# Sliding-window attention into a squared-ReLU FFN on one core: eight of the transposes of x moved from TensorE to transposing DMAs on ScalarE's queue

## The chip, the cores and the metric

The kernel runs on one core of one Trainium2 chip. The metric is device time in microseconds (us). Times of runs are medians over whole executions; times of single instructions come from one profiled execution and are counted from the start of its span. Engines: TensorE (PE), VectorE (DVE), ScalarE (ACT), GpSimd (POOL), SyncE (SP), which here only issues DMAs. ACT can issue DMAs too; such an instruction stands in the same queue as ACT's computing instructions, in order.

## The reference

Causal attention with a window of 64 over 8 sequences of 576 tokens (8 heads of 64), its output laid out as 4608 tokens x 512, and a feed-forward layer on it.

```python
scores = scale * q @ k.T                     # q, k, v: (8, 8, 576, 64)
mask = (rel >= 0) & (rel < 64)               # rel = query position - key position
attn = softmax(where(mask, scores, -1e9))
x = (attn @ v).transpose(0, 2, 1, 3).reshape(4608, 512)
h = maximum(x @ w_in, 0)                     # w_in: 512 x 2048
out = (h * h) @ w_out                        # w_out: 2048 x 512
```

## The kernel before

**Blocks.** The tokens are worked in nine blocks of 512. Blocks 0 to 7 are the first 512 tokens of each sequence; block 8 (`g == B`) holds the last 64 tokens of all eight. A block's attention has four units, one for each pair of heads: `(g, hp)` with `hp` 0 to 3.

**One unit.** `Sc` makes the scores of a unit on TensorE into one of two PSUM tiles, `at0` or `at1` (L287), and ACT takes their exponential into `pm` (L294). `M` applies the mask on DVE (L301). `AV` multiplies by v on TensorE into the same `at` tile (L317), `N` divides by the sums on DVE and leaves x of the unit as `xs` in SBUF (L327; three buffers). `X` transposes xs into `xT`, which the feed-forward layer needs with the features on the partitions: four TensorE transposes into the unit's own `at` tile (L343) and a copy by ACT from there (L124, called with the name `copy`). For block 8 only, `X` issues one transposing DMA on SP instead (L335).

**Feed-forward layer.** `F1(g, f)` computes 128 of the 2048 hidden features: four matmuls into `hps` (L357; two PSUM tiles), maximum with 0 by DVE into `hr` (L360; three buffers), square by ACT into h2 (L361). The second product, from block 2 on, is done with seven products of half size in each direction in place of eight (`L2S`, L444), with sums formed on DVE beforehand (`S_sum`, L420, and `T_sum`). The products go to two PSUM tiles, `chain` and `side`; ACT empties them into `osb` (L458) or DVE adds them there (L461). A product that writes `chain` anew has to wait for the eviction of the one before.

**Stages.** After a start that is written out, the loop `for n in range(1, NBLK)` makes stages 1 to 8. Stage n does the second product of block n, the first product of block n+1 and the attention of block n+2. The matmul groups of the two products alternate in a list `fill` of 30 groups, and the steps of the attention are put ahead of given groups with `put(i, ...)`. Two units run side by side (`t` = 0, 1), the first pair of a block from group 8 or 9 of its stage on, the second pair from group 19 or 20 (17 in stage 6). The order of all instructions is written by hand (`tc.manual_schedule()`); every engine runs its own instructions in that order.

**Loads.** `next_part`, called between groups, loads 128 tokens of q, k or v (SP, L211; L214 and L218 for block 8), has POOL cast them to fp16 (L126), and, for q and k, transposes them with a DMA on SP (`transpose_part`, L244), four parts behind the loading. In stage n it brings in block n+3: 12 loads and 8 transposes, for block 8 more (20 parts, 12 of them transposed). The stores of the output (L382) stand in SP's queue as well.

**Semaphores.** DMAs of SP and ACT use eight semaphores in turn (DMAHW0 to 7). What an instruction has to wait for is worked out from the tiles that it reads and writes when the program is built.

Of the kernel before, what the change touches and what calls it, by code (L numbers as in the profile page):

```python
# [15 lines left out]
def kernel(  # L16
# [13 lines left out]
    nc = tc.nc  # L30
    B, H, S, D = q.shape
# [22 lines left out]
    ps_tr = ctx.enter_context(tc.tile_pool(name="ps_tr", bufs=1, space=bass.MemoryType.PSUM))  # L54
# [67 lines left out]
    def copy(engine, out, in_):  # L122
        if engine is nc.scalar:
            engine.activation(out=out, in_=in_, func=AF.Copy, scale=1.0)  # L124
        else:
            engine.tensor_copy(out=out, in_=in_)  # L126
# [120 lines left out]
    pm, av, xs, xT = {}, {}, {}, {}  # L247
# [49 lines left out]
    def M(g, hp):  # L297
        p = pm[g, hp]
        m0 = 1 if g == B else 0
        m = mask[:, m0:m0 + 8, :].rearrange("p j r -> p (j r)")  # L300
        nc.vector.tensor_tensor(out=p[:], in0=p[:], in1=m.unsqueeze(1).broadcast_to([P, 2, 512]),  # L301
                                op=ALU.min)
# [24 lines left out]
        nc.vector.tensor_tensor(out=x[:].rearrange("p j h d -> p h j d"), in0=a[:, :, :, 0:D],  # L327
                                in1=rden[:].unsqueeze(3).broadcast_to([P, 2, 4, D]), op=ALU.mult)

    def X(g, hp, engine=nc.scalar, pool=ps_tr, tag="tr", own=None):  # L330

        if g not in xT:
            xT[g] = xtpool.tile([P, DMC, 512], FP16, name="xT", tag="xT")
        if g == B:
            nc.sync.dma_start_transpose(out=xT[g][:, hp, :].rearrange("p (j t) -> p j t", j=4),  # L335
                                        in_=xs[g, hp][:].rearrange("p j h d -> p (j h d)"))
            return
        if own is not None:
            tr = at_ps[own][:, 0, :].bitcast(FP16).rearrange("p (a b) -> p a b", a=2)
        else:  # L340
            tr = pool.tile([P, 2, 512], FP16, name="xtr", tag=tag)
        for jp in range(4):
            nc.tensor.transpose(out=tr[:, 0, jp * P:(jp + 1) * P], in_=xs[g, hp][:, jp, :, :],  # L343
                                identity=ident[:])
        copy(engine, xT[g][:, hp, :], tr[:, 0, :])
# [4 lines left out]
    def F1(g, f, pool=ps_f1, tag="f1", into=None):  # L350
        if g not in h2:
            h2[g] = h2pool.tile([P, FFC, 512], FP16, name="h2", tag="h2")
        hps, done = open_f1.pop((g, f), (None, 0))
        if hps is None:
            hps = into if into is not None else pool.tile([P, 512], FP32, name="hps", tag=tag)
        for c in range(done, DMC):
            nc.tensor.matmul(hps[:], w_in_sb[:, c, f * P:(f + 1) * P], xT[g][:, c, :],  # L357
                             start=(c == 0), stop=(c == DMC - 1))
        hr = opool.tile([P, 512], FP32, name="hr", tag="hr")
        nc.vector.tensor_scalar(out=hr[:], in0=hps[:], scalar1=0.0, scalar2=None, op0=ALU.max)  # L360
        nc.scalar.activation(out=h2[g][:, f, :], in_=hr[:], func=AF.Square)  # L361
# [26 lines left out]
    def F2(g, ts, quarter, pool, tag, into=None):  # L388
        if quarter == 0:
            f2[g, ts] = into if into is not None else pool.tile([P, 512], FP32, name="ops", tag=tag)  # L390
        for f in range(4 * quarter, 4 * quarter + 4):
            nc.tensor.matmul(f2[g, ts][:], h2[g][:, f, ts * P:(ts + 1) * P], w_out_sb[:, f, :],  # L392
                             start=(f == 0), stop=(f == FFC - 1))
        if quarter == 3:
            osb = opool.tile([P, DM], FP32, name="osb", tag="osb", bufs=5)
            nc.scalar.activation(out=osb[:], in_=f2[g, ts][:], func=AF.Copy, scale=OUT_SCALE)
            to_store.append(lambda: store(g, ts, osb))
        if quarter == 1:
            while to_store:
                to_store.pop(0)()  # L400
# [21 lines left out]
    def T_sum(k):  # L422
        if k == 1:
            minus(t_of(1), b_of(0, 1), b_of(0, 0))
        elif k == 2:
            minus(t_of(2), b_of(1, 1), t_of(1))
        elif k == 3:
            minus(t_of(3), b_of(1, 1), b_of(0, 1))
        else:
            minus(t_of(4), b_of(1, 0), t_of(2))  # L430

    def S_sum(g, k, s):
        if k == 1:
            minus(s_of(1, s), a_of(g, 1, 0, s), a_of(g, 1, 1, s), ALU.add)
        elif k == 2:
            minus(s_of(2, s), s_of(1, s), a_of(g, 0, 0, s))
        elif k == 3:
            minus(s_of(3, s), a_of(g, 0, 0, s), a_of(g, 1, 0, s))
        else:
            minus(s_of(4, s), a_of(g, 0, 1, s), s_of(2, s))  # L440
# [74 lines left out]
    with tc.manual_schedule():  # L515
# [18 lines left out]
        dve, pool, act = nc.vector, nc.gpsimd, nc.scalar  # L534
# [127 lines left out]
        def A(g, hp, i=1):  # L662
            AV(g, hp, i)
            N(g, hp)
# [38 lines left out]
        for n in range(1, NBLK):  # L703
            g = seq[n]
            last = n == NBLK - 1
            one = None if last else seq[n + 1]
            if n == 1:
                second = [lambda ts=ts, i=i: F2(g, ts, i, None, None, into=(chain, side)[ts % 2])
                          for ts in range(4) for i in range(4)]
            elif last:  # L710
                more = [ps_f1.tile([P, 512], FP32, name="more", tag="f1") for _ in range(2)]
                banks = [(more[0][:, 0:HC], more[1]), (chain[:, 0:HC], side)]
                second = [lambda p=p, s=s: L2S(g, p, s, banks[s])
                          for p, s in ((1, 0), (2, 0), (1, 1), (6, 0), (2, 1), (5, 0), (7, 0),
                                       (6, 1), (3, 0), (4, 0), (5, 1), (7, 1), (3, 1), (4, 1))]
            else:
                second = [lambda p=p, s=s: L2S(g, p, s, (chain[:, 0:HC], side))
                          for s in range(2) for p in ORDER]
            first = [] if last else [lambda f=f: F1(one, f) for f in range(FFC)]
            order = ("22222222" + 8 * "112" if n == 1 else  # L720
                     "2" * 14 if last else
                     "1212121212121211" + "21212121121122")
            a, b = iter(first), iter(second)
            fill = [next(a if c == "1" else b) for c in order]
            at = {}

            def put(i, *work):
                at.setdefault(i, []).extend(work)

            if n == 1:  # L730
                put(0, lambda: Sc(g2, 3), lambda: A(g2, 2))
                put(2, lambda: M(g2, 3))
                put(3, lambda: X(g2, 2, own=1))
                put(5, lambda: A(g2, 3))
                put(7, lambda: X(g2, 3, own=1))
                for i, k in ((1, 1), (3, 2), (6, 3), (8, 4)):
                    put(i, lambda k=k: T_sum(k))
            else:
                for i, k, s in (((0, 1, 1), (0, 2, 1), (2, 4, 0), (3, 3, 1), (4, 4, 1)) if last else
                                ((2, 4, 0), (4, 1, 1), (6, 2, 1), (9, 3, 1), (13, 4, 1))):  # L740
                    put(i, lambda k=k, s=s: S_sum(g, k, s))
            if not last:
                end = len(fill) - 1
                put(24 if n == 1 else 17, lambda: S_sum(one, 3, 0))
                put(end if n == 1 else end - 1, lambda: S_sum(one, 1, 0))
                put(end, lambda: S_sum(one, 2, 0))
            base = 4 * (n + 2)
            for i, two in zip((11, 21) if n == 1 else (9, 20) if n == 2 else (9, 17) if n == 6 else (8, 19),
                              (units[base:base + 2], units[base + 2:base + 4])):
                for t, u in enumerate(two):  # L750
                    if u is not None:
                        put(i, lambda u=u, t=t: Sc(*u, i=t))
                        put(i + 3 + t, lambda u=u: M(*u))
                        put(i + 6, lambda u=u, t=t: A(*u, i=t))
                        put(i + (7 if u[0] == B else 8 + t), lambda u=u, t=t: X(*u, own=t))
            for i, group in enumerate(fill):
                for work in at.pop(i, []):
                    work()
                total = 12 + (30 * (n - 1) + i + 1) * (len(load_list) - 12) // 140
                while done < total and (parts_left or pending):  # L760
                    next_part()
                    done += 1
                group()
            assert not at, at.keys()
# [30 lines left out]
```

## Time and profile before

| | |
|---|---|
| Median of 3 runs | 302.12 us (301.2 to 302.79) |
| The profiled execution: time, span | 301.14 us, 298.8 us |
| Busy: PE, DVE, ACT, POOL | 289.0, 216.6, 169.2, 126.0 us |
| Transposes of xs on PE (L343) | 128 matmuls, 88 of them into `at` |
| Copies xT by ACT from `at` (L124) | 22, 586 ns each |
| Transposing DMAs, all on SP | 52 of q and k (L244), 4 of xs (L335) |
| DMA queue 1 | 143504 packets, 55.14 MB |

The span is the time from the first to the last instruction of the program; the rest of an execution's time lies around it. A line of a view gives line number, engine, operation, output <- input. A queue's own instructions (SPq, ACTq), DMA issues above all, are not counted as busy. In the listings by line, three numbers with slashes are the shortest, median and longest duration in ns. In a timeline the first number is the start in us, the second the length; xN means that N like instructions stand together.

### The profile page before, as it was taken

The numbers are of one execution on the slowest core, as the hardware profiler recorded it, in microseconds if no ns is written. First come the engines' busy times: TensorE is split into PE (matmuls) and PEld (weight loads), VectorE is DVE, ScalarE is ACT, GpSimd is POOL, SyncE is SP. The second block draws the span as 40 slices with busy tenths as digits, with TensorE's granted clock in tenths as the row PEclk, the third lists the DMA queues.
The fourth block names the chain that finished last, engine by engine and source line by source line (L and its number), as shares of the span: only waits on it lengthen the run. The fifth ranks groups of instructions, "written<-read, shape, count | busy, mean of one in ns | idle before, by whom it ended". The sixth has DMA issues, their size and how long they took to land.

```text
span 298.8 us, 7389 instructions
## 1 busy us (share of the span) xinstructions
PE 289.0 (97%) x2908; PEld 181.0 (61%) x2908; DVE 216.6 (72%) x380; ACT 169.2 (57%) x291; POOL 126.0 (42%) x214
## 2 busy tenths in 40 slices
PE   7999998999999999999999999999999999999994
PEld 5544544545444456666666666666666666766783
DVE  4677527588866777968797879787878688875651
ACT  3657745587466557565656565656565655444521
POOL 4568849963383367339326634723241000000001
PEclk9999999999999999999999999999999999999999
DMA  7999999999999995999899999999994023200016
GB/s 217 249 344 378 391 335 270 308 204 172 190 256 174 199 218 107 206 191 219 164 210 244 197 178 224 173 202 208 220 205 145 2 37 105 74 36 35 2 70 140
DMA packets 143874, 56.05 MB, mean 188 GB/s; under 512 B 127904, under 2 KB 136352, under 8 KB 143840
## 3 DMA queue, kind: packets, MB, share of 16 engines
q1 hardware_dynamic: 143504, 55.14, 85.8%
q8 instruction: 22, 0.36, 0.5%
q0 software_dynamic: 96, 0.26, 0.4%
q10 hardware_dynamic: 240, 0.20, 0.3%
q14 instruction: 12, 0.10, 0.1%
HBM read 38.80 MB, written 9.44 MB: 161 GB/s over the span
## 4 chain that ended last, share of the span: by engine, by line
PE 77%; DVE 1%; ACT 1%; issue 1%; DVEq 0%
PE hps L357 36%; PE chain L444 15%; PE side L444 11%; PE at L317 3%; PE at L287 3%; PE side L392 2%; PE chain L392 2%; PE more L444 2%; PE at L343 1%; DVE hr L360 0%; PE tr L256 0%; ACT h L361 0%; PE hps L373 0%; ACT xT L124 0%; PE at L357 0%
## 5 line engine op out<-in xcount | busy, mean ns | idle before, releaser
L361 ACT ACTIVATE h<-hr 128x512 f16<-128x512 f32 x144 | 90.2, 631 | 93.8 <-DVE hr L360 93.7
L357 PE MATMUL hps<-xT,w_in_sb 128*128 128x512 f16 x560 | 138.7, 379 | 0.2
L360 DVE TENSOR_SCALAR hr<-hps 128x512 f32<-128x512 f32 x143 | 97.0, 687 | 40.8 <-PE hps L357 38.3
L357 PEld LDWEIGHTS <-w_in_sb 128*128 128x128 f16 x564 | 52.7, 98 | 46.7 <-issue 1.4
L444 PEld LDWEIGHTS <-hsum 128*128 128x128 f16 x448 | 43.2, 98 | 13.2
L126 POOL CAST v_ev<-st_v 128x512 f16<-128x512 f32 x32 | 22.6, 706 | 41.7 <-DMA st_v<-in_v_dram 41.7
L444 PEld LDWEIGHTS <-h 128*128 128x128 f16 x336 | 32.6, 98 | 9.3
L126 POOL CAST k<-st_k 128x512 f16<-128x512 f32 x31 | 21.7, 703 | 35.0 <-DMA st_k<-in_k_dram 31.9
L294 ACT ACTIVATE pm<-at 128x1024 f16<-128x1024 f32 x35 | 34.2, 1020 | 2.8 <-PE at L287 2.8
L386 POOL DMA_DIRECT2D out_dram<-osb x2 | 1.3, 632 | 66.1 <-ACT osb L458 66.1
L444 PE MATMUL chain<-wsum,hsum 128*128 128x256 f16 x208 | 27.0, 273 | 0.0
L327 DVE TENSOR_TENSOR xs<-at,rden 128x512 f16<-128x512 f32 x36 | 24.9, 692 | 1.2
L301 DVE TENSOR_TENSOR pm<-pm,mask 128x1024 f16<-128x1024 f16 x32 | 23.8, 755 | 1.8 <-ACT pm L294 1.8
L420 DVE TENSOR_TENSOR hsum<-h 128x1024 f16<-128x1024 f16 x28 | 20.4, 729 | 6.0 <-ACT h L361 5.7
L126 POOL CAST q<-st_q 128x512 f16<-128x512 f32 x27 | 18.5, 706 | 12.4 <-DMA st_q<-in_q_dram 7.2
L235 POOL CAST v_od<-st_v 64x512 f16<-64x512 f32 x30 | 21.4, 713 | 1.6
L392 PEld LDWEIGHTS <-h 128*128 128x128 f16 x128 | 11.8, 98 | 12.8
L458 ACT ACTIVATE osb<-chain 128x256 f32<-128x256 f32 x39 | 14.6, 375 | 5.6 <-PE chain L444 5.6
L317 PEld LDWEIGHTS <-pm 128*64 128x64 f16 x576 | 11.5, 110 | 8.2 <-issue 3.2
L124 ACT ACTIVATE xT<-at 128x512 f16<-128x512 f16 x22 | 12.8, 586 | 4.0 <-PE at L343 4.0
L317 PE MATMUL at<-v_ev,pm 128*64 128x65 f16 x384 | 14.6, 198 | 0.3 <-ACT h L361 0.3
L392 PE MATMUL ops<-w_out_sb,h 128*128 128x512 f16 x64 | 14.8, 380 | 0.0
(95 smaller groups left out, 319.6 us busy)
## 6 DMA issues: line engine op xcount, KB each, us to landing
st_k<-in_k_dram SPq DMA_DIRECT2D x35, 256.0 KB, 4.0
out_dram<-osb SPq DMA_DIRECT2D x32, 256.0 KB, 3.1
st_v<-in_v_dram SPq DMA_DIRECT2D x28, 256.0 KB, 4.4
st_q<-in_q_dram SPq DMA_DIRECT2D x26, 256.0 KB, 4.9
st_w<-in_moe_w_out_dram SPq DMA_DIRECT2D x10, 256.0 KB, 5.3
w_st<-in_moe_w_in_dram SPq DMA_DIRECT2D x4, 512.0 KB, 6.3
wsum<-in_moe_w_in_dram SPq DMA_DIRECT2D x6, 256.0 KB, 8.2
st_v<-in_v_dram SPq DMA_DIRECT2D x10, 128.0 KB, 5.7
```

What stands on the lines that cost most here:

```text
L126: engine.tensor_copy(out=out, in_=in_)
L235: nc.gpsimd.tensor_copy(out=od[g][to:to + 64, m, :, 0:D], in_=st["v", g, c][of:of + 64, :].rearrange("p (h d) -> p h d", h=H))
L294: nc.scalar.activation(out=p[:, hh, :] if apart else p[:], in_=sc[hh] if apart else both[:], func=AF.Exp, scale=1.0 / float(D) ** 0.5)
L301: nc.vector.tensor_tensor(out=p[:], in0=p[:], in1=m.unsqueeze(1).broadcast_to([P, 2, 512]), op=ALU.min)
L317: nc.tensor.matmul(a[jj * 64:(jj + 1) * 64, hh, jp * VW:jp * VW + D + 1], pm[g, hp][:, hh, j * 64:(j + 1) * 64], vsel, start=True, stop=True)
L327: nc.vector.tensor_tensor(out=x[:].rearrange("p j h d -> p h j d"), in0=a[:, :, :, 0:D], in1=rden[:].unsqueeze(3).broadcast_to([P, 2, 4, D ...
L357: nc.tensor.matmul(hps[:], w_in_sb[:, c, f * P:(f + 1) * P], xT[g][:, c, :], start=(c == 0), stop=(c == DMC - 1))
L360: nc.vector.tensor_scalar(out=hr[:], in0=hps[:], scalar1=0.0, scalar2=None, op0=ALU.max)
L361: nc.scalar.activation(out=h2[g][:, f, :], in_=hr[:], func=AF.Square)
L392: nc.tensor.matmul(f2[g, ts][:], h2[g][:, f, ts * P:(ts + 1) * P], w_out_sb[:, f, :], start=(f == 0), stop=(f == FFC - 1))
L420: (engine or nc.vector).tensor_tensor(out=out, in0=a, in1=b, op=op)
L444: nc.tensor.matmul(to, a[:, f, :], b[:, f, :], start=start and f == 0, stop=f == HF - 1, skip_group_check=True)
```

## The change

In blocks 4 to 7, `X` of units 0 and 1 no longer transposes on TensorE. It issues one transposing DMA, SBUF to SBUF, on ACT's queue. Units 2 and 3 of these blocks and all units of blocks 1 to 3 stay on TensorE; block 8 stays on SP's queue. The place of `X` in the order of the program is the same.

```diff
-    def X(g, hp, engine=nc.scalar, pool=ps_tr, tag="tr", own=None):
+    def X(g, hp, engine=nc.scalar, pool=ps_tr, tag="tr", own=None, queue=None):
...
-        if g == B:
-            nc.sync.dma_start_transpose(out=xT[g][:, hp, :].rearrange("p (j t) -> p j t", j=4),
-                                        in_=xs[g, hp][:].rearrange("p j h d -> p (j h d)"))
+        if queue is not None:
+            queue.dma_start_transpose(out=xT[g][:, hp, :].rearrange("p (j t) -> p j t", j=4),
+                                      in_=xs[g, hp][:].rearrange("p j h d -> p (j h d)"))
             return
...
-                        put(i + (7 if u[0] == B else 8 + t), lambda u=u, t=t: X(*u, own=t))
+                        queue = nc.sync if u[0] == B else nc.scalar if u[0] > 3 and u[1] < 2 else None
+                        put(i + (7 if u[0] == B else 8 + t),
+                            lambda u=u, t=t, queue=queue: X(*u, own=t, queue=queue))
```

That is eight units: the first pair of the attention in stages 2 to 5.

## The prediction

> **What bounds the kernel now.** I read the page first: busy times and the chain that ended last.
>
> ```profile
> PE 289.0 (97%) x2908; PEld 181.0 (61%) x2908; DVE 216.6 (72%) x380; ACT 169.2 (57%) x291; POOL 126.0 (42%) x214
> ...
> PE 77%; DVE 1%; ACT 1%; issue 1%; DVEq 0%
> ```
>
> TensorE is busy from end to end and carries the chain. ScalarE (ACT) at 57% has spare time on average, but TensorE depends on it: ACT squares h and empties the PSUM tiles `chain` and `side`, in the order of its queue. A hold in that queue comes through once TensorE needs a tile that ACT has not emptied.
>
> The views by line give what is removed (L343) and the price of what replaces it (L244, L335, so far on SyncE, SP).
>
> ```profile
> L343 PE MATMUL at<-ident,xs x88: 219/219/219, 76.9 to 225.4; 128*128 128x128 f16 x88
> ...
> L244 SPq DMA_TRANSPOSE qT<-q x24: 1195/1217/3296, 63.7 to 197.9; - x24
> ...
> DMA to landing us min/median/max: 3.1/3.7/5.8
> ...
> L335 SPq DMA_TRANSPOSE xT<-xs x4: 1195/1206/2004, 242.8 to 252.2; - x4
> ```
>
> A transposing DMA holds its issuing queue 1.2 us (3.3 us the first time of all) and lands 3.7 us (3.1 to 5.8) after its issue began; the four of L335, on a quiet ring, took 2.4 to 4.0.
>
> Next the timeline of ACT where x of block 4's first two units is copied in stage 2, and of SP in the same stretch.
>
> ```profile
> 125.39 0.36 ACT L458 ACTIVATE osb<-chain 128x256 f32<-128x256 f32 x1
> 125.66 0.59 ACT L124 ACTIVATE xT<-at 128x512 f16<-128x512 f16 x1
> 126.14 0.63 ACT L361 ACTIVATE h<-hr 128x512 f16<-128x512 f32 x1
> 126.67 0.58 ACT L124 ACTIVATE xT<-at 128x512 f16<-128x512 f16 x1
> ...
> 128.63 1.92 ACT L294 ACTIVATE pm<-at 128x1024 f16<-128x1024 f32 x2
> 130.44 0.39 ACT L458 ACTIVATE osb<-chain 128x256 f32<-128x256 f32 x1
> ```
>
> ```profile
> 130.85 1.44 SPq L244 DMA_TRANSPOSE kT<-k  x1
> ...
> 137.20 1.08 SPq L211 DMA_DIRECT2D st_k<-in_k_dram  x1
> 140.74 1.99 SPq L244 DMA_TRANSPOSE qT<-q  x1
> ```
>
> In the program, the eight transposes of block 5's q and k stand ahead of x of block 4. SP runs late against that order: it issues the last of them (kT) at 130.85, when ACT is already past its copy at 125.66.
>
> **What the built program adds.** The queues of the changed program show one thing that the diff does not. The first ACT transpose of each pair waits for the DMA semaphores of all SP transposes recorded ahead of it, to the end of their transfers; SP's next q transpose then waits for both ACT transposes to land. The two queues take turns. In the program of before, with all transposes on SP, no such wait exists. The Trainium skill has the reason (DMA: Bandwidth & Descriptors, section "Silent corruption: two transposing streams in flight at once"): transposes issued from SP and from ACT must not be in flight together, and the later stream must wait for the earlier one's full completion. It speaks against this change; no run here shows what happens without it.
>
> **Removed.** 32 transposing matmuls and eight copies. From the starts of its neighbours a set of four holds TensorE about 0.22 us (212.71 to 212.93): 0.44 a stage, 1.8 in all. The copies free ACT for 8 x 0.586 = 4.7 us, off the path.
>
> **Added, stage 2.** ACT reaches the DMA after the eviction that ends at 125.75. It may go when kT of 130.85 has landed: 130.85 + 3.7 = 134.55, a hold of 8.8. Queued behind it are a square, the second DMA, a square, two exponentials and the eviction of `chain`: 134.55 + 1.2 + 0.63 + 1.2 + 0.63 + 1.92 + 0.39 = 140.5. TensorE waits for that eviction:
>
> ```profile
> 130.46 1.89 PE L357 MATMUL hps<-xT,w_in_sb 128*128 128x512 f16 x8
> 132.19 1.04 PE L444 MATMUL chain<-wsum,hsum 128*128 128x256 f16 x8
> ```
>
> The product at 132.19 writes `chain`, which was emptied by 130.83. It now starts at 140.5: 8.3 us later, with the saved 0.44 already lost in the wait. Two hps tiles and three hr tiles let TensorE come as far as 132, no farther.
>
> **The clock after the gap.** No idle stretch of TensorE in this trace is over 0.6 us between its first matmul and its last, so the price of one of 8 us is not shown. The nearest row is the start:
>
> ```profile
> 5.27 0.63 PE L98 MATMUL busy<-maskb,ident 128*128 128x512 f16 x1
> ...
> 7.70 0.38 PE L98 MATMUL busy<-maskb,ident 128*128 128x512 f16 x1
> ```
>
> The same matmul takes 0.63 at 5.27 and 0.38 at 7.70; the change falls near 6.2, 4.7 us after the first matmul at 1.43, and slow ones start twice as far apart (0.43 against 0.22). Bounds: nothing, if the pause is too short, or half of 4.7 = 2.35. I take 2.0 after stage 2, near the only row that follows an idle engine. For the 4 us of stage 5, half as long, I take 0.5. The Trainium skill (TensorE: Matmul & The Clock Gate, "What's actually happening") lets the clock fall to half after an idle window of about 3.4 us and come back after as long; by it each of the two pauses would cost about 1.7, my estimate from its figure, and the sum below would be 15.0.
>
> **Stages 3 and 4.** In stage 3 ACT reached x at 155.08 before, now at 163 to 165; SP's last kT there was issued at 157.00 and lands at 160.7, SP having no part in the delay. No hold. The two DMAs cost ACT 2 x (1.2 - 0.586) = 1.2 us more; the next evictions of `chain` (159.56 before, needed at 162.75) and the masks (started 160.23 and 161.02, their exponentials ended 157.85 and 158.77) have room for that. TensorE gains 0.44. Stage 4 is alike: last kT issued at 181.21, x at 184.94. Together -0.9. What these stages cost falls on SP: its first q transpose of the next block has to wait for ACT's second DMA to land, and from there its chain starts.
>
> **Stage 5.** Count from X6, the moment ACT reaches x of block 6 in stage 4. The second DMA is issued after 1.2 + 0.38 and lands 3.7 later: 5.3. Then SP runs the transposes of block 8, twelve instead of eight:
>
> ```profile
> 190.32 1.71 SPq L244 DMA_TRANSPOSE qT<-q  x1
> ...
> 216.47 1.21 SPq L244 DMA_TRANSPOSE k2T<-k  x1
> ```
>
> 26.15 from first to last issue, and 3.7 to land: ready at X6 + 35.1. ACT reaches x of block 7 at 214.71 - 184.94 = 29.8, less 0.4, so X6 + 29.4: a hold of 5.7. Behind it in ACT's queue is an eviction of `chain`:
>
> ```profile
> 214.71 0.58 ACT L124 ACTIVATE xT<-at 128x512 f16<-128x512 f16 x1
> 215.19 0.38 ACT L458 ACTIVATE osb<-chain 128x256 f32<-128x256 f32 x1
> ```
>
> TensorE needs `chain` at 217.32, 2.5 after ACT comes to x at 214.8; the eviction now ends at 5.7 + 1.2 + 0.38 = 7.3. Loss 4.8. Bounds: if SP runs its 11 steps without the waits of before (1.94 each, 204.86 to 206.80, and two pairs of stores at about 1.1), 23.5 in place of 26.15, the loss is 2.2; if the DMA lands after 5.8, 6.9. I take 4.2, since part of SP's waits should go. SP's later loads slip by some 8 us, hidden by block 8's scores, which start at 235.1 in the trace of before, 14.9 after the last k2T would have landed (220.2).
>
> **Sum:** 8.3 + 2.0 + 4.2 + 0.5 - 0.9 = 14.1. The profiled execution took 301.14 (span 298.8), so 315.2; the median of the three runs shown is 302.12, 1.0 above it, which makes 316.
>
> **Rivals.**
> *Only the first hold.* SP catches up in stage 5: its sequence contracts and the DMA lands in 2.4, so ACT finds k2T landed or nearly so. For: the slack of 2.5 and SP's own waits. Against: twelve transposes at 1.94 are 21 us of pure issue. Time: 302.1 + 8.3 + 2.0 - 1.3 = 311.1.
> *Faster: no hold at all.* ACT comes to x after SP's transposes have landed, and only the removed matmuls count: 302.1 - 1.8 = 300.3. It decides at one point, whether the last kT of stage 2 lands before ACT's 125.7; SP would have to be 9 us earlier than the trace has it, and nothing ahead of that point is changed. Without the waits between the queues it would be this too.
> *Heavier.* The first ACT transpose costs 3.3 us as SP's first did (+2.1), landings take 5.8 in both holds (+4.2 at most), the clock drops after both (+2.2): 302.1 + 14.1 + 8.5, up to 324.7.
>
> **Chances.** Both holds, near the sum: 0.64 (its own range 312 to 320). First hold alone: 0.2. Heavier: 0.11. No hold: 0.04, and 0.01 for an end within 0.5%, about what a measurement of this kernel can tell from no change. The range of 309 to 321 takes in the first two and part of the third.
>
> **What would show it.** Right: 56 L343 matmuls into `at` in place of 88, eight DMA_TRANSPOSE on ACT's queue; ACT idle about 9 us near 126 to 135 with SP's kT as the releaser; TensorE idle near 132 to 140, then slow matmuls and a lower PEclk; no such gap in stages 3 and 4; SP idle ahead of its first q transposes in stages 4 and 5 by several us; a second gap of about 4 us in stage 5. Wrong: no gap in stage 2 (the waits do not bind), gaps in all four stages (SP is slowed by more than I think), or clock at full speed after the gap (the 2.5 fall away).

## The result, and the profile after

| | before | after |
|---|---|---|
| median (6 runs each) | 302.64 us (301.2 to 303.8) | 320.54 us (318.0 to 322.31) |
| ratio | | 1.0589, 95% interval 1.0535 to 1.0643 |
| profiled execution: time, span | 301.14, 298.8 us | 322.31, 320.6 us |

17.9 us slower by the medians. The profiled executions differ by 21.2, since the one of before is the fastest of its six and the one of after the slowest. What follows is the account of these two. Ratios, here and below, leave out runs that are over 1.5% above the fastest of their kernel, so they can differ a little from the quotients of the medians.

The page of the changed kernel: busy times, the 40 slices of TensorE and of its granted clock, and the chain that ended last.

```profile
PE 291.0 (91%) x2876; PEld 179.9 (56%) x2876; DVE 216.8 (68%) x380; ACT 165.8 (52%) x283; POOL 122.8 (38%) x214
...
PE   7898998999999999639999998999539999999994
...
PEclk9999999999999999969999999999959999999999
...
PE 55%; DMA 10%; SPq 8%; DVE 3%; ACT 2%; issue 2%; POOL 1%; ACTq 1%; DVEq 0%
```

TensorE falls from 97% of its span to 91%. The loss is not spread: two places in the row of digits have a hole (63 and 53), and the clock dips at both. The chain no longer is TensorE alone; DMA and SP's queue carry 18% of it.

The view of line 335, with the transposing DMAs on both queues (first and last start at the end):

```profile
L335 ACTq DMA_TRANSPOSE xT<-xs x8: 1204/1216/1942, 136.1 to 237.2; - x8
...
DMA to landing us min/median/max: 2.4/6.5/7.8
```

TensorE has 2876 matmuls in place of 2908: 32 transposes less, 56 of L343 into `at` in place of 88. The issue holds ACT for 1.2 us as it held SP, but the eight DMAs of ACT take 6.3 to 7.8 us to land (the four of SP, in the same line, 2.4).

**Stage 2.** SP's last transpose recorded ahead of ACT's DMA, ACT's timeline, then TensorE's:

```profile
132.26 1.44 SPq L244 DMA_TRANSPOSE kT<-k  x1
```

```profile
126.98 0.36 ACT L458 ACTIVATE osb<-chain 128x256 f32<-128x256 f32 x1
136.07 1.31 ACTq L335 DMA_TRANSPOSE xT<-xs  x1
137.43 0.63 ACT L361 ACTIVATE h<-hr 128x512 f16<-128x512 f32 x1 [10.08 <-DMA out_dram<-osb]
...
141.29 0.39 ACT L458 ACTIVATE osb<-chain 128x256 f32<-128x256 f32 x1
```

```profile
141.73 1.87 PE L444 MATMUL chain<-wsum,hsum 128*128 128x256 f16 x8 [8.23 <-ACT osb L458]
```

ACT has nothing to compute for 10 us, issues the DMA at 136.07, and the eviction of `chain` ends at 141.7. The wait is put down to a store's DMA in the bracket; by the landing times in the trace, the last of the semaphores that the DMA waits for is that of SP's kT, issued at 132.26 and landed at 135.97. A second wait lies beneath this one: the semaphore that ACT's DMA was to use had a load of v to finish, which landed at 133.87. TensorE stands idle for 8.23 us, and its product takes 1.87 instead of 1.04. The windows (length; then busy time of PE, PEld, DVE, ACT, POOL; granted clock; DMA share; GB/s) show the clock:

```profile
139.00:146.00 7.00, 4.27 (x46) 2.64 (x46) 4.84 (x10) 4.61 (x8) 4.59 (x7) 0.57 1.09 158
146.00:153.00 7.00, 7.00 (x56) 4.94 (x54) 5.41 (x10) 4.04 (x8) 1.46 (x2) 1.00 0.94 183
```

**Stage 4.** Here it was no transpose but a semaphore that held ACT's first DMA. ACT was done with its squares at 196.05:

```profile
197.61 1.21 ACTq L335 DMA_TRANSPOSE xT<-xs  x1
198.94 0.38 ACT L458 ACTIVATE osb<-chain 128x256 f32<-128x256 f32 x1 [2.89 <-DMA st_q<-in_q_dram]
198.96 1.20 ACTq L335 DMA_TRANSPOSE xT<-xs  x1
```

The last kT had landed at 195.41; the load of q on the semaphore whose turn it was landed at 197.43. TensorE lost 1.25 us.

**Stage 5.** SP first: from the first q transpose of block 8 to the last k2T, and in the list of SP's waits the line that is new. Then ACT and TensorE.

```profile
198.57 0.68 SPq L218 DMA_DIRECT2D st_k<-in_k_dram  x1
206.45 1.23 SPq L244 DMA_TRANSPOSE qT<-q  x1
...
232.29 1.49 SPq L244 DMA_TRANSPOSE k2T<-k  x1
```

```profile
SPq L244 <- DMA xT<-xs: 17.0, 4, 7.1
```

```profile
225.80 1.23 ACT L361 ACTIVATE h<-hr 128x512 f16<-128x512 f32 x2 [1.98 <-DVE hr L360]
235.91 1.21 ACTq L335 DMA_TRANSPOSE xT<-xs  x1
```

```profile
237.65 1.86 PE L444 MATMUL chain<-wsum,hsum 128*128 128x256 f16 x8 [8.39 <-ACT osb L458]
```

SP stands from 199.3 to 206.45 for ACT's DMAs of stage 4 to land, comes to its last k2T 16 us later than before (216.47), and ACT in turn stands from 227.0 to 235.9. The last k2T landed at 235.89; the load on the semaphore that ACT's DMA was to use had landed at 233.64.

**The account.** How much later TensorE starts the same work after than before:

| work of TensorE | before | after | later by | added |
|---|---|---|---|---|
| stage 2, hps | 130.46 | 131.60 | 1.14 | 1.59 before the change acts, -0.45 matmuls removed |
| stage 2, `chain` behind the hold | 132.19 | 141.73 | 9.54 | 8.40 hold |
| stage 2, `side` | 135.75 | 146.75 | 11.00 | 1.46 half clock |
| stage 4, hps | 186.67 | 197.24 | 10.57 | -0.43 in stages 3 and 4 up to here |
| stage 4, `chain` | 187.55 | 199.37 | 11.82 | 1.25 short hold |
| stage 5, hps | 216.44 | 228.22 | 11.78 | -0.04 |
| stage 5, `chain` behind the hold | 217.32 | 237.65 | 20.33 | 8.55 hold |
| stage 5, `side` | 219.06 | 240.84 | 21.78 | 1.45 half clock |
| last `chain` of the program | 293.58 | 315.36 | 21.78 | 0 |

The spans differ by 21.75. Without the 1.59 us of the start, the change costs 20.2 us in these two executions, 2.3 more than by the medians: the sizes below are those of one execution.

### The profile page after: what moved, and what is told of

Its sections match the earlier page's. It is cut to its first block, busy times and chain, and to the rows that moved or that the text cites. A ratio compares the mean times of both kernels' runs of the same rounds, so it can differ in the third digit from the quotient of the medians.

```text
span 320.6 us, 7342 instructions
## 1 busy us (share of the span) xinstructions
PE 291.0 (91%) x2876; PEld 179.9 (56%) x2876; DVE 216.8 (68%) x380; ACT 165.8 (52%) x283; POOL 122.8 (38%) x214
## 3 DMA queue, kind: packets, MB, share of 16 engines
q10 hardware_dynamic: 4592, 1.25, 2.9%
## 4 chain that ended last, share of the span: by engine, by line
PE 55%; DMA 10%; SPq 8%; DVE 3%; ACT 2%; issue 2%; POOL 1%; ACTq 1%; DVEq 0%
PE hps L357 25%; PE chain L444 11%; PE side L444 8%; SPq L244 6%; DMA st_v<-in_v_dram 4%; PE at L317 2%; DMA xT<-xs 2%; PE side L392 2%; PE chain L392 2%; PE more L444 2%; PE at L287 2%; DMA st_k<-in_k_dram 1%; DVE hr L360 1%; DMA st_q<-in_q_dram 1%; SPq L218 1%
## 5 line engine op out<-in xcount | busy, mean ns | idle before, releaser
L357 PE MATMUL hps<-xT,w_in_sb 128*128 128x512 f16 x560 | 140.3, 381 | 2.1 <-DVE hr L360 0.9
L444 PE MATMUL chain<-wsum,hsum 128*128 128x256 f16 x208 | 28.7, 284 | 17.7 <-ACT osb L458 17.7
L126 POOL CAST v_ev<-st_v 128x512 f16<-128x512 f32 x32 | 21.5, 670 | 46.8 <-DMA st_v<-in_v_dram 46.8
L444 PEld LDWEIGHTS <-h 128*128 128x128 f16 x336 | 32.8, 98 | 10.2
L301 DVE TENSOR_TENSOR pm<-pm,mask 128x1024 f16<-128x1024 f16 x32 | 24.8, 778 | 10.7 <-ACT pm L294 10.5
L458 ACT ACTIVATE osb<-chain 128x256 f32<-128x256 f32 x39 | 14.5, 373 | 19.5 <-DMA st_v<-in_v_dram 10.2
L126 POOL CAST q<-st_q 128x512 f16<-128x512 f32 x27 | 17.7, 672 | 17.4 <-DMA st_q<-in_q_dram 14.6
L461 DVE SCALAR_TENSOR_TENSOR osb<-side,osb 128x256 f32<-128x256 f32 x26 | 11.0, 421 | 15.7 <-ACT osb L458 13.0
L235 POOL CAST v_od<-st_v 64x512 f16<-64x512 f32 x30 | 20.7, 690 | 1.6
```

The source lines that it names most:

```text
L235: nc.gpsimd.tensor_copy(out=od[g][to:to + 64, m, :, 0:D], in_=st["v", g, c][of:of + 64, :].rearrange("p (h d) -> p h d", h=H))
L444: nc.tensor.matmul(to, a[:, f, :], b[:, f, :], start=start and f == 0, stop=f == HF - 1, skip_group_check=True)
```

## The experiments

Theory A: the loss is the order between two transposing queues. ACT waits for SP's late transposes, SP for ACT's landings, and ACT's other work stands behind its wait. Rival B: the transposing DMAs cost by themselves, so the loss goes by their number. All edits below are made in the changed kernel's line that chooses the queue, unless another line is shown. Medians are given beside those of the kernel before in the same job.

### The same DMAs on SP's queue (sp_queue)

```diff
-queue = nc.sync if u[0] == B else nc.scalar if u[0] > 3 and u[1] < 2 else None
+queue = nc.sync if u[0] == B or u[0] > 3 and u[1] < 2 else None
```

> The same eight transposing DMAs, issued on SyncE's queue instead of ScalarE's. Theory A (the loss is the order between two transposing queues: ScalarE is held until SyncE's late transposes have landed): with one queue no transpose waits for the other queue, so no hold on ScalarE and no gap of TensorE of 8 us; 301 to 305 us, the upper part if xs (three buffers) comes free too late because SyncE issues the DMA some 9 us behind. Rival B (the DMA transposes themselves cost: their traffic and their landing times): the same eight transposes are made beside the same loads, so most of the 17.9 us stays, 312 us or more.

Measured: 308.72 us beside 301.85, ratio 1.0215 (1.0171 to 1.026). No gap in stages 2 to 4; one in stage 5, and DVE's list of waits names it:

```profile
DVE xs L327 <- DMA xT<-xs: 6.2, 2, 5.4
```

308.72 lies between the two expected ranges. The holds on ACT are gone, so it was not the transfers themselves that made them. But a new wait came, larger than expected: SP is so late in stage 5 that DVE waits 5.4 us for an xs buffer, TensorE 4.5 us, with the clock falling on top.

### One block at a time (only_b4, only_b5, only_b7)

```diff
-queue = nc.sync if u[0] == B else nc.scalar if u[0] > 3 and u[1] < 2 else None
+queue = nc.sync if u[0] == B else nc.scalar if u[0] == 4 and u[1] < 2 else None    # 5 and 7 in the other two
```

> Only block 4 (stage 2) uses ScalarE's queue, two DMAs instead of eight. Theory A: the whole first hold (TensorE gap 8.2 us, 1.7 us of half clock) and nothing after it: 302.6 + 9.9 = 312.5 us (311 to 314). Rival B (cost goes by the number of transposes): a quarter of 17.9, 307 us.

> Only block 5 (stage 3) uses ScalarE's queue. In the changed kernel this stage had no hold. Theory A (SyncE runs late against ScalarE, and the first hold had let it catch up): SyncE's last kT of the stage lands near 160.7, ScalarE comes to its DMA near 155.2, so a hold of 5.5; the eviction of chain ends 7.1 after ScalarE's arrival, TensorE needs it 2.5 after: loss 4.6, plus 0 to 1.7 for the clock: 307 to 309 us. Rival (stage 3 is harmless by itself, as in the changed kernel): 302 to 302.6 us.

> Only block 7 (stage 5) uses ScalarE's queue, so SyncE's transposes of block 8 wait for nothing beforehand. Theory A (half of the second gap comes from SyncE having waited for ScalarE's landings in stage 4): k2T lands near 220.2, ScalarE comes at 214.8, hold 5.4, TensorE loses 4.5 and 0 to 1.7 for the clock: 307 to 309 us. Rival (stage 5 has its own price, the gap of 8.4 and 1.5 of clock stay whole): 312.5 us.

Measured, beside 301.85: 310.24 (ratio 1.0271, 1.0214 to 1.0328), 307.14 (1.0151, 1.008 to 1.0222), 308.01 (1.019, 1.0133 to 1.0248). Two DMAs cost 5.3 to 8.4 us by the medians, each block by itself. The runs of only_b5 lie far apart (304.01 to 308.28 us). Block 5, harmless in the changed kernel, is not harmless alone; TensorE's gap there:

```profile
162.89 1.03 PE L444 MATMUL chain<-wsum,hsum 128*128 128x256 f16 x8 [3.50 <-ACT osb L458]
```

So the first hold had shielded stage 3, as theory A says. Block 7 alone has a gap of 3.86 where the changed kernel had 8.39; here ACT's hold lasts until SP's last k2T has landed (220.44, the DMA is issued at 220.58), and the DMA's own semaphore was free before that. Block 4 alone stayed 2 us under the expectation: its gap was 5.77 in the profile, because SP was that much earlier in this execution (ACT's DMA is issued at 133.90 in place of 136.07).

### Blocks 4 and 7, without 5 and 6 (b4_b7)

```diff
-queue = nc.sync if u[0] == B else nc.scalar if u[0] > 3 and u[1] < 2 else None
+queue = nc.sync if u[0] == B else nc.scalar if u[0] in (4, 7) and u[1] < 2 else None
```

> Blocks 4 and 7 on ScalarE's queue (stages 2 and 5), blocks 5 and 6 on TensorE as before, so SyncE's transposes in stages 4 and 5 wait for no landing on ScalarE's ring. Theory A (the second gap comes from SyncE having to start from ScalarE's landing in stage 4): after the first hold TensorE is some 8 us later and SyncE is not, k2T lands near 220.3, ScalarE comes near 222.8: no second hold, 310 to 311 us, as only_b4. Rival (stage 5 has its own price whatever went before): 310.2 + 5.4 or more, 315 to 318 us.

Measured: 312.11 us beside 303.01, ratio 1.0312 (1.0265 to 1.0359). The only long gap is that of stage 2 (7.89 us). In stage 5 SP issues its last k2T at 219.43 and ACT comes to its DMA at 226.69: nothing to wait for. After a first hold, the second gap of the changed kernel is therefore made by the DMAs of blocks 5 and 6, through SP's waiting for them; their own stages hardly show it. This run does not tell the two blocks apart. The time is 1 us over the expectation: the clock stayed at half for 10.2 us here, and from `chain` to `side` it took 6.17 us, 2.61 more than before (1.46 in the changed kernel).

### TensorE work put into the gaps (fill_gap, fill_right)

```diff
-        for c in range(done, DMC):
-            nc.tensor.matmul(hps[:], ...)
+        for again in range(8 if (g, f) in ((5, 13), (8, 10)) else 1):
+            for c in range(done, DMC):
+                nc.tensor.matmul(hps[:], ...)
```

The matmul's other arguments are left out here. fill_right has (3, 13) and (6, 10) in place of the two pairs.

> The changed kernel, with one group of four matmuls of the first product done eight times over (the result overwritten each time) just ahead of the product that waits in stage 2, and the same in stage 5: 6.05 us of extra TensorE work inside each of the two gaps of 8.2 and 8.4 us. If the clock is what follows from the idle stretch (1.7 us after the first, 1.5 us after the second), the gaps left are 2 us, the clock stays up and the time falls by about 3 us, to 317 to 318 us. If the half clock costs nothing, or does not come from the idle stretch: unchanged, 320 to 321 us; where a hold is shorter than 6 us, the rest of the filling is added.

The block numbers were wrong: stage n makes the first product of block n+1, so the 6.05 us went into stages 4 and 7. Measured: 325.42 us beside 302.71, ratio 1.0764 (1.0724 to 1.0804). It says nothing of the clock, but something of the second hold: 12.1 us of work were added and the time rose by 4.9 against the changed kernel. The 6 us in stage 4, ahead of ACT's next meeting with SP, were got back:

```profile
235.33 1.03 PE L445 MATMUL chain<-wsum,hsum 128*128 128x256 f16 x8 [2.43 <-ACT osb L459]
```

The gap of 8.39 is one of 2.43: SP had the time to catch up, and the clock did not fall there.

> The filling as meant for fill_gap, now at the groups that stand just ahead of the waiting products (block 3's first product in stage 2, block 6's in stage 5): 6.05 us of extra TensorE work inside each gap. If the half clock follows from the idle stretch: the gaps shrink to 2 us, the clock stays up, and the time falls by 1.7 + 1.5 = 3.2 us to some 317.5 us. If the clock costs nothing: 320.5 us; where a hold is shorter than 6 us, the rest of the filling is added.

Measured: 318.11 us beside 303.01, ratio 1.0475 (1.0414 to 1.0537). In stage 2 the gap shrank to 0.82 and the clock stayed up:

```profile
140.40 1.03 PE L445 MATMUL chain<-wsum,hsum 128*128 128x256 f16 x8 [0.82 <-ACT osb L459]
...
143.95 1.04 PE L445 MATMUL side<-w_out_sb,hsum 128*128 128x256 f16 x8
```

From this `chain` to this `side` it is 3.55 us, as before (3.56); in the changed kernel 5.02. That is the 1.46 of the account. In stage 5 a gap of 2.40 was left, and the clock fell all the same, so only half of the gain could come. The interval touches that of the changed kernel, so the medians alone do not show the clock's price; it rests on the distances in the traces.

### Four DMAs instead of eight (one_unit)

```diff
-queue = nc.sync if u[0] == B else nc.scalar if u[0] > 3 and u[1] < 2 else None
+queue = nc.sync if u[0] == B else nc.scalar if u[0] > 3 and u[1] < 1 else None
```

> Only unit 0 of blocks 4 to 7 on ScalarE's queue, four DMAs instead of eight. Theory A: the first hold stays (8.3, less 0.6), SyncE waits in stage 4 for one landing instead of two, some 3 us earlier, and the second gap shrinks by as much: 315 to 317 us. Rival (cost by the number of DMAs): half of 17.9, 311.6 us. To be seen as well: whether one DMA alone lands in less than the 6.3 to 7.8 us of two.

Measured: 318.75 us beside 303.01, ratio 1.0498 (1.044 to 1.0555). Half the DMAs cost 15.7 us, not half of 17.9: B falls. It is above the 315 to 317 of theory A. Unit 1 is now copied by ACT out of `at1` behind the hold, and TensorE's next scores into `at1` wait for that, ahead of where it waited for `chain`:

```profile
136.24 0.61 PE L287 MATMUL at<-qT,kT 64*128 64x64 f16 x16 [7.04 <-ACT xT L124]
```

The gap of stage 5 is 4.38, about half; some 3 us less than 8.39 was expected. One DMA alone lands after 5.0 to 6.1 us, little less than one of two.

### The DMAs later in ACT's order (b4_later)

```diff
-queue = nc.sync if u[0] == B else nc.scalar if u[0] > 3 and u[1] < 2 else None
-put(i + (7 if u[0] == B else 8 + t),
+queue = nc.sync if u[0] == B else nc.scalar if u[0] == 4 and u[1] < 2 else None
+put(i + (7 if u[0] == B else 13 + t if queue is not None else 8 + t),
```

> only_b4 with its two DMAs five groups later in the program: behind the two exponentials and one eviction of chain instead of ahead of them. Theory A (the price is set by what is queued behind the held DMA): ScalarE reaches it at 131.4 instead of 125.8, is held 3.2 instead of 8.8, and what follows is an eviction of side that TensorE needs at 135.75: loss 0.5 to 1, 302.5 to 304 us. Rival (the transposes cost by themselves): 310 us as only_b4.

Measured: 313.82 us beside 303.01, ratio 1.0364 (1.0328 to 1.0401). The expectation failed. The first DMA behaved as said: issued at 135.11, no gap of TensorE at the product that waited before. The second did not:

```profile
135.11 1.32 ACTq L335 DMA_TRANSPOSE xT<-xs  x1
...
144.75 1.21 ACTq L335 DMA_TRANSPOSE xT<-xs  x1
```

I had overlooked that five groups later a q transpose of SP stands between the two. It was issued at 140.22, after the first had landed (140.14), and the second DMA had to wait for it, to 144.73. Two changes of turn instead of one, 8 us for ACT, and x arrives so late that block 4's first product waits 4.7 us for it.

### ACT's ring without loads beside it (b8_act)

```diff
-queue = nc.sync if u[0] == B else nc.scalar if u[0] > 3 and u[1] < 2 else None
+queue = nc.scalar if u[0] == B else None
```

> The kernel before, with only the four DMA transposes of block 8 moved from SyncE's to ScalarE's queue, in stage 6, where no loads and no other transposes are under way. If ScalarE's ring is as fast as SyncE's and its 5.0 to 7.8 us of landing in the changed kernel come from sharing the engines with SyncE's loads: 2.4 to 4 us to land, as on SyncE there. If the ring itself is slower: 5 to 7 us. The time of the kernel: 302 to 304 us, since ScalarE waits in its queue for VectorE's xs.

Measured: 303.99 us beside 302.71, ratio 1.0049 (1.0013 to 1.0086). The view of line 335:

```profile
L335 ACTq DMA_TRANSPOSE xT<-xs x4: 1206/1288/1649, 244.2 to 254.6; - x4
...
DMA to landing us min/median/max: 2.4/2.6/3.2
```

Where no loads run beside it, ACT's queue is as fast as SP's was there (2.4 to 4.0).

### Two tries at a version without the holds (sp_b4to6, sp_xs5)

```diff
-queue = nc.sync if u[0] == B else nc.scalar if u[0] > 3 and u[1] < 2 else None
+queue = nc.sync if u[0] == B or 3 < u[0] < 7 and u[1] < 2 else None     # sp_b4to6
```

```diff
-x = apool.tile([P, 4, 2, D], FP16, name="xs", tag="xs", bufs=3)         # sp_xs5, on top of sp_queue
+x = apool.tile([P, 4, 2, D], FP16, name="xs", tag="xs", bufs=5)         # and stp with 9 buffers for 10
```

> The transposing DMAs on SyncE's queue as in sp_queue, but not for block 7: its first pair goes back to TensorE. In sp_queue the one new gap (4.5 us, and 6.8 us of half clock around it) stood in stage 5, where SyncE came to x of block 7 late and VectorE waited 5.4 us for a free xs buffer. Theory A (that buffer wait is all that sp_queue lost): no gap, three pairs at 0.44 us gained less nothing: 300.5 to 302 us. Rival B (the transposes cost in every stage): 306 us or more.

> sp_queue with five xs buffers in place of three (and nine staging tiles in place of ten, for room). Theory A (VectorE waited for an xs buffer): the gap of stage 5 goes, 300 to 302.5 us; the ninth staging tile may cost the start some tenths. Rival (the gap comes from SyncE's late loads or the clock, not from xs): 307 us or more.

Measured, beside 302.71: sp_b4to6 303.64, ratio 1.0017 (0.9984 to 1.0049); sp_xs5 307.05, ratio 1.0116 (1.0063 to 1.0169). The first is no faster: in the profiled execution the wait for xs stands in stage 4 (TensorE idle 2.64 us). The runs of the second go from 303.54 to 308.52 us, and the profiled one is the slowest. In it the buffer wait is gone and another has its place, for x itself: TensorE waits 4.94 us for a transposing DMA, since SP comes to block 7's transposes at 229.6 and the first product of that block wants them at 228.5. What the faster runs waited for is not shown. No version beat the kernel before.

## Why the prediction was right, and where not

Forecast 316.0 in a range of 309 to 321, 0.95 for slower; measured 320.54. The case was the one called likeliest, both holds; the time lies 0.5 us above the range given for that case alone (312 to 320). The mechanism was right. Of the terms of the sum, the second hold was taken at half its size, and stages 3 and 4 had the wrong sign.

- **The turn between the queues and the first hold.** Right in place: 8.3 forecast, 8.40 measured in this execution; SP's kT landed 3.71 after its issue, forecast 3.7. That the size agrees to 0.1 us is luck: TensorE's gap, 8.23 here, was 5.77, 7.14 and 7.89 in only_b4, fill_gap and b4_b7, which are the same program up to that point. That ACT is held by DMAs of SP and not by its own transfers is shown by sp_queue (the same DMAs, no hold on ACT) and by stage 5 of b4_b7 (SP's transposes landed, no hold); that the transposes end the hold, by the landings (135.97, 235.89, and 220.44 in only_b7).
- **A wait that the prediction did not have.** The eight semaphores are shared with the loads, and a DMA waits for the one before it on its semaphore. In stages 2 and 5 this alone would have held ACT until 133.87 and 233.64: 6.5 of the 8.7 us and 6.6 of the 8.9 us that it stood. This is read from the landings; no run separates the two waits there.
- **Removed.** 0.45 in stage 2 and 0.43 in stage 4, forecast 0.44 each. In stages 3 and 5 nothing was gained: TensorE now waited 0.33 and 0.25 us for `hr`, which it did not before, so that after the place of the transposes it was 11.18 us late (11.00 ahead of it) and 11.79 (11.82).
- **The clock.** Forecast 2.0 and 0.5, measured 1.46 and 1.45. The first was taken too large from the start of the program, the second too small because the second gap was. In only_b4 and b4_b7 the same stretch of stage 2 cost 2.76 and 2.61, so a middling price was not known to better than 1 us. The Trainium skill's rule (TensorE: Matmul & The Clock Gate, "What's actually happening") lets the clock come back after about 3.4 us of work, from which the prediction had estimated 1.7 for each pause, nearer for both in this execution. The trace agrees that the clock falls to half and is back 3.4 us after work resumes (141.7 to 145.1); in only_b4 it took 6.0 us (139.4 to 145.3), and pauses of 2.40 and 2.64 us were enough for the fall (last section), so here the measurement decides.
- **Stages 3 and 4: the sign failed.** Forecast -0.9, measured +0.78 from the row of `side` in stage 2 to the row of hps in stage 5. Stage 3 had no hold, as said, but no gain either. In stage 4 ACT, free at 196.05, could issue only at 197.61, since the semaphore had to wait for the load of q: 1.25 us for TensorE. I had counted the waits for transposes alone.
- **Stage 5: the step that failed was the landing after X6.** "Lands 3.7 later: 5.3" was 10.3: 1.56 for the semaphore, 1.35 to the second issue, 7.36 to land in place of 3.7. From there on the steps hold: 25.84 from the first q transpose to the last k2T (forecast 26.15), 3.60 to land (3.7). So SP was ready at X6 + 39.8 (forecast 35.1), ACT was there at X6 + 31.0 (29.4), and TensorE lost 8.55, forecast 4.8 and then shaded to 4.2, on the ground that part of SP's waits would go; only 0.3 of them went. That SP's start is what counts is shown by b4_b7 (second gap gone) and fill_gap (gap down to 2.43).
- **What made 7.4 of 3.7** is shown in part. Beside SP's loads ACT's transposes took 6.3 to 7.8 us in the changed kernel and 2.4 to 7.2 in the other runs; in stage 6 without loads 2.4 to 3.2 (b8_act). The same eight transfers on SP's queue (sp_queue) took 2.4 to 5.2 beside the loads of the same stages, 3.70 and 2.77 in stage 4. So neither ACT's queue nor the loads make it alone; it takes both. How the two queues share the DMA engines was not tried and stays open.
- **The rivals.** One hold alone: wrong for this kernel, though b4_b7 is exactly that case, at 312. Faster: SP's lateness excluded it (its kT landed 8.6 us after ACT came). The prediction added that without the waits between the queues the kernel would be 1.8 faster. No run shows that: with the DMAs on SP, and no turn between queues, it is 6.9 slower, as SP has no room for eight more transposes, and on ACT the shared semaphores would have held it all the same. Heavier: neither the cold first issue (1.31 us in place of 3.3) nor landings of 5.8 in the holds came (3.71 and 3.60); the second fall of the clock did, and the long landing came where no case had it, in stage 4.

## What to carry to other kernels

In this program a transposing DMA on a second queue takes turns with the transposes of the first, to the end of their transfers, and with every DMA that used its semaphore before it. If the one queue runs late against the program and the other computes, everything behind the DMA on the computing engine waits for that lateness. Before moving a transfer, compare where each queue stands in time at that point of the program, and count which transfers of the other queue are recorded ahead of it and between. Moving the DMAs onto the late queue is no way out by itself, since they need issue time there: here SP, some 9 us behind ACT at both holds, had none to give.

## What the runs showed of the hardware

A pause of TensorE of 2.4 to 2.6 us can halve the clock. In sp_b4to6 TensorE was idle for 2.64 us (194.94 to 197.57), and these are the windows around it (the granted clock is the third number from the end):

```profile
194.00:197.00 3.00, 0.94 (x6) 0.20 (x3) 0.17 (x1) 0.00 (x0) 2.83 (x6) 1.00 1.11 155
197.00:200.40 3.40, 2.83 (x16) 2.10 (x17) 2.30 (x5) 1.92 (x4) 1.10 (x2) 0.50 1.10 191
```

The half clock lasts 3.4 us and lies mostly behind the pause; from 200.4 on the clock is full again (0.99 to 204). A pause of 2.40 (fill_right) did the same, one of 2.43 (fill_gap) did not, so at this length the pause's length does not decide. In all runs the half clock inside the kernel lasts 3.4, 6.8 or 10.2 us, one, two or three times 3.4. Stretches of fixed length would fit both facts, and it would then count when a pause falls; no run tests that.
